# Query weights summed during K/V, and one of four gate-times-up products on GpSimd, in a fused attention and feed-forward kernel

## The chip, the core and the metric

The kernel runs on one core of a Trainium2 chip. The metric is the device time of one execution in microseconds (us). The engines are named as in the profile: PE is TensorE, DVE is VectorE, ACT is ScalarE, POOL is GpSimd, SP is SyncE, whose queue issues all DMAs here.

## What is computed

A layer norm feeds a linear attention of 32 heads and a gated feed-forward network; the attention's output is multiplied by SiLU of the feed-forward output and added to the input. There are 2048 tokens, D = 1024 and F = 3584, in bf16.

```python
xn = layernorm(x)
q, k, v = heads(xn @ wqkv)                  # 32 heads of 32
phi = lambda t: where(t > 0, t + 1, exp(t)) + 1e-6
kv = einsum("bhsd,bhse->bhde", phi(k), v);  z = phi(k).sum(over tokens)
o = (phi(q) @ kv) / (phi(q) . z + 1e-6)
s = o @ wo
f = (silu(xn @ w_gate) * (xn @ w_up)) @ w_down
out = x + s * silu(f)
```

## The kernel before, in words

**Strassen products.** All large matrix products go through one or two levels of a Strassen-like scheme with seven products in place of eight. So each block of weights needs sums and differences of its quarters before TensorE can use it. `WF` (line 607 on) holds a block: 8 KB per partition of raw weights, 8 KB of outer sums (`combos`, line 639: four operations of 128x1024) and 6 KB of inner sums (`inner`, line 648: eight operations of 128x256 or 128x512). `wload` (line 1239) issues the two DMAs of a block and its outer sums, and rotates through three raw places (`raw_at`, line 1234), three places for outer sums (`cmb_at`, line 1235) and two for inner sums. Query blocks (`q_load`) are summed on DVE, outer and inner. Gate/up blocks (`gu_load`) are summed on POOL, except the outer sums of block 0, which are on DVE.

**Stages.** (1) K/V, 0 to about 115 us of the profiled span: token tiles are normalised, transposed and multiplied with the K and V weights, and the sum of phi(k) times v is kept in PSUM. (2) Queries: two weight blocks times two halves p of the tokens, four "pairs" (`q_pair`), each with its phi (`phi_evac`, line 1035: ACT's exponential, then DVE's L1038 and L1045 or an addition). In between the K/V sum is scaled (L1210), transposed, multiplied with wo (`m_build`) and stored to DRAM as the M product; `den_run` (line 1278) makes the denominators and reciprocals, once for each half of the heads. (3) Gate/up: 14 blocks n times two token halves p, 28 pairs (`gu_pair`, line 1336), z counting them. Each product of gate and up is stored to DRAM. Beside pairs z = 3 to 10 runs `normalise` (line 1305), which divides the queries by their denominators: per call four scalings on ACT and four DVE products of 128x512 from SBUF alone. (4) The normalised queries times M, `s_pair`, from about 525 us. (5) The down projection from about 574 us, which loads chunks of the gate-times-up products (`h_load`) and multiplies with w_down; its `d_pair` makes the output.

**A pair and its four evacuations.** A pair writes a 2 x 2 arrangement of 128x512 results for gate and again for up. Three of the four are read from PSUM (kind "ps"), and one, from Strassen product 7, was first combined by DVE into an SBUF tile of f32 (kind "sb"). For gate, ACT applies SiLU; for up, line 1351 multiplies with the SiLU tile, in place and on DVE, and a DMA stores the tile.

**What sets the order.** Nothing is issued in the order of the code. Every operation becomes an `Op` of a `Plan`, with its engine, assumed duration, what it reads and writes, and the PSUM bank or temporary buffer that it takes from a pool. `schedule` (line 125) gives each a due time from TensorE's order and places them by engine, earliest start first, then due time; `emit` (line 261) writes each engine's list with the semaphore waits. A DMA that is not `asap` is also tied to a matmul some 12 us before its due time. For the planner, DVE work on SBUF alone ("port") waits for POOL. In `op` (line 460) every reader of a PSUM bank counts as a writer of it, so that two reads of a bank always follow one another with a wait, on one engine too.

**Memory.** A region from 80 KB on (`W0`) holds the weights; during K/V it also holds K/V sums, x tiles (112 to 120 KB), normalised tiles (124 to 130 KB) and phi(k) tiles. In stage 5 the same region takes chunks of products (`HC`, `HT`, `H2`: places in KB) and inner sums (`HI_AT`, `WI_AT`); `cur` (line 1618) says which chunk place each quarter takes.

The planner's calls for the two stages in question:

```python
Q[0] = q_load(0)
...
q_pair(0, 0, Q[0])
Q[1] = q_load(1)
...
G[0] = gu_load(0)
G[0].inner(IE, JG)
```

Of the kernel before, what the change touches and what calls it, by code (L numbers as in the profile page):

```python
# [9 lines left out]
ALU = mybir.AluOpType  # L10
F32 = mybir.dt.float32
BF16 = mybir.dt.bfloat16
FP16 = mybir.dt.float16
# [48 lines left out]
class Plan:  # L62
# [11 lines left out]
        self.lead = lead  # L74
        self.tag = None

    def op(self, eng, reads, writes, fn, busy, sem=None, nbytes=0, urgent=0.0, cow=None, after=None, vbs=(), asap=False):
        o = Op()
        o.eng, o.fn, o.busy, o.sem, o.nbytes, o.urgent, o.asap = eng, fn, busy, sem, nbytes, urgent, asap
        o.lat = 0.0 if sem is not None else self.LAT[eng]  # L80
        o.idx = len(self.ops)
        o.tag = self.tag
        o.port = False
        o.pad = 0.0
        o.vbs = []
        for v in vbs:
            if v not in o.vbs:
                o.vbs.append(v)
                v.ops.append(o)
        preds = set()  # L90
        for r in reads:
            for k in r.keys:
                preds.update(self.lastw.get(k, ()))
        if cow is not None:
            preds.update(cow.preds)
        if after is not None:
            preds.add(after)
        for r in writes:
            for k in r.keys:
                if cow is None:  # L100
                    preds.update(self.lastw.get(k, ()))
                    preds.update(self.readers.get(k, ()))
        for r in reads:
            for k in r.keys:
                self.readers.setdefault(k, []).append(o)
        for r in writes:
            for k in r.keys:
                if cow is None:
                    self.lastw[k] = [o]
                    self.readers[k] = []  # L110
                else:
                    self.lastw[k].append(o)
        preds.discard(o)
        o.preds = preds
        o.succs = []
        for p in preds:
            p.succs.append(o)
        o.pecum = self.pecum
        if eng == "pe":
            self.pecum += busy  # L120
            self.lastpe = o
        self.ops.append(o)
        return o

    def schedule(self):
# [58 lines left out]
        while len(order) < total:  # L184
            best = None
            for e in self.ENGS:
                a = avail[e]
                if not a:
                    continue
                t = free[e]  # L190
                lim = None
                if e == "pe":
                    n = 0
                    for o in pe_next:
                        if n >= self.window:
                            lim = o.idx
                            break
                        n += 1
                pick = None
                for o in a:  # L200
                    if lim is not None and o.idx >= lim:
                        continue
                    when, got = place(o, t)
                    if got is None:
                        continue
                    if o.port:
                        when = max(when, free["pool"])
                    if e == "pe":
                        key = (0.0, o.idx) if when <= t + 0.05 else (when, o.idx)
                    else:  # L210
                        key = (0.0, o.dl, o.idx) if when <= t else (when, o.dl, o.idx)
                    if pick is None or key < pick[0]:
                        pick = (key, o, when, got)
                if pick is None:
                    continue
                s = max(t, pick[2])
                if best is None or s < best[0]:
                    best = (s, e, pick[1], pick[3])
            if best is None:
                raise RuntimeError("no operation can go on: " + "; ".join(  # L220
                    "%s %d" % (o.eng, o.idx) for e in self.ENGS for o in avail[e][:4]))
            s, e, o, got = best
            for v, k in got:
                v.slot = k
                v.pool.free.discard(k)
                v.pool.pend.remove(o.idx)
                o.preds = o.preds | set(v.pool.users[k])
            o.start = s
            if o.sem is not None:
                free[e] = s + o.busy  # L230
                dma_free = max(s, dma_free) + o.nbytes / 310e3
                o.done = max(s + o.nbytes / 190e3, dma_free) + 1.2 + o.pad
            else:
                if o.port:
                    s = max(s, free["pool"])
                    free["pool"] = max(free["pool"], s + o.busy)
                free[e] = s + o.busy
                o.done = s + o.busy + o.lat
            for v in o.vbs:
                v.left -= 1  # L240
                if v.left == 0:
                    P = v.pool
                    P.free.add(v.slot)
                    P.time[v.slot] = max(q.done for q in v.ops)
                    P.users[v.slot] = list(v.ops)
                    P.armed[v.slot] = v.leaves
            avail[e].remove(o)
            if e == "pe":
                done.add(o)
                while pe_next and pe_next[0] in done:  # L250
                    pe_next.popleft()
            order.append(o)
            for q in o.succs:
                q.npred -= 1
                q.ready = max(q.ready, o.done)
                if q.npred == 0:
                    avail[q.eng].append(q)
# [43 lines left out]
def build_kernel(nc, A_x, A_wqkv, A_wo, B_w_gate, B_w_up, B_w_down, out, WINDOW=20, NWARM=12, NIDLE=5, LEAD=12.0):  # L301
# [9 lines left out]
    UBANK, PU = 0.0, 6.0  # L311
    RQ = lambda w, i, j, kind: kind == "ps"
    RK = lambda q, c, kind: c == 0
    N0, NA, WA = 3, 2, True
    GC0 = ("dve",) * 4
    XE0 = XE1 = XE2 = XE3 = "dve"

# [8 lines left out]
    with ExitStack() as es:  # L326
# [133 lines left out]
        def op(eng, reads, writes, fn, busy, hold=(), **kw):  # L460
            rr, rv = split(reads)
            wr, wv = split(writes)

            mine = [v for v in rv if v.pool is BANK]
            wr += [v.r for v in mine if v not in wv]
            if mine:
                kw["urgent"] = kw.get("urgent", 0.0) + UBANK
            return PL.op(eng, rr, wr, fn, busy, vbs=rv + wv + list(hold), **kw)
# [762 lines left out]
                vsem(s), 128 * KB, asap=True)  # L1231


        raw_at = [W0 * KB, (W0 + 8) * KB, R2 * KB]
        cmb_at = [(W0 + 16 + 8 * k) * KB for k in range(3)]
        inn_at = [(W0 + 40 + 6 * k) * KB for k in range(2)]
        wk = [0]

        def wload(srcs, ceng, ieng, dt=BF16, reads=()):
            k = wk[0]  # L1240
            wk[0] += 1
            rk = (0, 1, 0)[k] if k < 3 else 2 - k % 3
            f = WF(raw_at[rk], cmb_at[k % 3], inn_at[k % 2], dt)
            for q, src in enumerate(srcs):
                if not isinstance(src, list):
                    src = [(slice(0, 8), src)]
                for kts, sr in src:
                    dma(list(reads), [f.raw_r(q, range(kts.start, kts.stop))], f.v[:, q, kts], sr,
                        dsem("wr%d_%d_%d" % (rk, q, kts.start)), 512 * KB // len(src), asap=WA)
            f.combos(ceng)  # L1250
            if ieng:
                f.inner(ieng, JQ)
            return f
# [82 lines left out]
        def gu_pair(p, n, wf, at=()):  # L1336
            sgs = {}

            def evac(w, i, j, src, v, kind):
# [7 lines left out]
                if kind == "ps" and UPACT:  # L1347
                    u = tmp(H1)
                    act([v], [u], partial(vap, u, FP16), src, ACT.Identity, 512)
                    v, src, fast = u, partial(vap, u, FP16), True  # L1350
                tt([v, s], [s], partial(vap, s, FP16), src, partial(vap, s, FP16), ALU.mult, 512, fast)
                dma([s], [named("h", p, f)], h_scr[p, f][:, n * 512:(n + 1) * 512], partial(vap, s, FP16), vsem(s),
                    128 * KB, asap=True, cow=hcow(p, f))
            ST.pair(Pair(Prov(wf, XV[p]), evac, JG), at)
# [68 lines left out]
                tt([x[1], y[1]], [z[1]], z[0], x[0], y[0], alu, (hi - lo) * 512, True)  # L1423


        HC = [80, 112, 199, 96, 87]
        HT = [119, 122.5, 103, 106.5]
        H2 = 103
        HI_AT = [73.5, 75.25, 77, 94, 110, 129.5, 194, 195.75]
        WI_AT = [70, 160, 163.5, 126, 119, 122.5]  # L1430
        gone = [VB(F2, only=k) for k in range(2)] + [VB(H1, only=k) for k in range(8, 12)]
        GB = 3584

# [3 lines left out]
        def hpart(o, w, lo=0, hi=14):  # L1437

            keys = []
            for n in range(lo, hi):  # L1440
                keys += (SB.reg(o * KB + n * 512, 512) if w is None else SB.reg(o * KB + n * 512 + w * 256, 256)).keys
            v = hchunk(o)[:, lo:hi]
            return (v if w is None else v[:, :, w * 128:(w + 1) * 128]), Region(keys)

# [139 lines left out]

        for z, (n, p) in enumerate(order):
            at = []
            if z == 0:
                at.append(partial(den_run, 1))
            gu_pair(p, n, G[n], at)
            if z == 0:  # L1590
# [24 lines left out]
                G[15 + u].inner(IS, JS)  # L1615
        ST.flush()

        cur, spare = [0, 2, 1, 3], 4

        def load(q, f, c):  # L1620
            if q < 4:
# [120 lines left out]
```

## Time and profile before

| what | value |
|---|---|
| median of 13 runs | 748.37 us (745.8 to 751.18) |
| the profiled execution, its own time | 750.71 us |
| span of the profiled execution | 749.0 us |
| granted TensorE clock, mean | 0.991 |
| busy: PE, DVE, ACT, POOL | 713.4, 588.1, 380.4, 260.6 us |

The span is what the profile covers, and the execution's time is 1.7 us longer. Busy time is the time in which an engine has at least one instruction under way. A row of a group gives line, engine, operation, output and inputs with shapes, how many, busy time and mean ns of one, and then the engine's idle time just before these instructions with what ended most of it. Since helpers record operations, most tensor operations have the line of the helper: L424 (matmuls), L474 (ACT), L482 (two-tensor operations on DVE and POOL). A row of the timeline gives start, duration, engine, line, operation and how many were merged, and in brackets the idle time before it and its releaser.

### The profile page before, as it was taken

The page shows a single profiled execution, that of the slowest core. Times are in us where ns is not written, and L with a number is a line of the kernel's source. Part 1 is how long each engine was busy: PE and PEld are TensorE (multiplying, and loading weights), DVE is VectorE, ACT ScalarE, POOL GpSimd, SP SyncE. Part 2 cuts the span into 40 slices and gives each one's busy share as a digit, 9 for nine tenths or more (in the row PEclk, how much of TensorE's full clock was granted, in tenths as well). Part 3 has the DMA queues.
Part 4 walks back from the last instruction along what each step waited for, and adds up shares of the span by engine and source line. Part 5 has one row for each costly group of instructions (what it writes and reads, how often), then busy time and mean ns, then how long its engine had stood idle before and what let it go on. Part 6 is the DMA issues. An engine that isn't in the chain of part 4 may idle for free.

```text
span 749.0 us, 11806 instructions
## 1 busy us (share of the span) xinstructions
PE 713.4 (95%) x4247; PEld 399.8 (53%) x4247; DVE 588.1 (79%) x1127; ACT 380.4 (51%) x729; POOL 260.6 (35%) x230
## 2 busy tenths in 40 slices
PE   8999998997898899999999999999999999999996
PEld 3444444443565555656666566656554455464642
DVE  5999665889899889888888888889978966556433
ACT  3778665886646567665455454544665122021211
POOL 2011000255528547856678655712740000000000
PEclk9999999999999999999999999999999999999998
DMA  9834205131133454467321333235699256463622
GB/s 305 200 86 102 39 0 169 58 113 32 44 117 112 155 195 138 154 231 226 106 84 59 106 99 118 90 111 169 187 323 286 71 174 202 137 197 100 187 71 70
DMA packets 141978, 101.57 MB, mean 136 GB/s; under 512 B 19040, under 2 KB 137056, under 8 KB 141920
## 3 DMA queue, kind: packets, MB, share of 16 engines
q1 hardware_dynamic: 141920, 100.82, 44.7%
q8 instruction: 33, 0.54, 0.3%
q14 instruction: 25, 0.20, 0.1%
HBM read 68.16 MB, written 29.49 MB: 130 GB/s over the span
## 4 chain that ended last, share of the span: by engine, by line
PE 70%; DVE 14%; DMA 6%; ACT 5%; issue 3%; SPq 0%; DVEq 0%; ACTq 0%
PE ps L424 70%; DVE SB L482 10%; ACT SB L474 4%; DMA SB<-h_scratch 2%; DVE ps L482 2%; DMA out_dram<-SB 1%; DVE SB L1038 1%; DMA SB<-in_A_x_dram 1%; DMA SB<-q_scratch 1%; ACT ps L474 1%; DVE SB L1045 1%; DMA m_scratch<-SB 0%; SPq L494 0%; DMA SB<-SB 0%; DVE SB L1210 0%
## 5 line engine op out<-in xcount | busy, mean ns | idle before, releaser
L424 PE MATMUL ps<-SB 128*128 128x512 f16 (+4 forms) x4126 | 704.0, 332 | 22.8 <-DVE ps L482 7.7
L424 PEld LDWEIGHTS ps<-SB 128*128 128x128 f16 (+1 forms) x4126 | 394.2, 98 | 330.4 <-DVE ps L482 17.0
L482 POOL TENSOR_TENSOR SB<-SB 128x1024 f16<-128x1024 bf16 (+3 forms) x196 | 246.3, 1283 | 234.1 <-PE ps L424 114.1
L474 ACT ACTIVATE SB<-ps 128x256 f32<-128x256 f32 (+5 forms) x443 | 234.9, 562 | 145.2 <-PE ps L424 114.5
L482 DVE TENSOR_TENSOR SB<-SB 128x512 f16<-128x512 f16 (+11 forms) x360 | 237.4, 694 | 56.0 <-ACT SB L474 23.1
L482 DVE TENSOR_TENSOR SB<-ps,SB 128x256 f32<-128x256 f32 (+2 forms) x318 | 181.6, 591 | 56.4 <-PE ps L424 44.7
L482 DVE TENSOR_TENSOR ps<-ps,SB 128x512 f32<-128x512 f32 (+1 forms) x250 | 128.1, 527 | 26.6 <-PE ps L424 16.9
L474 ACT ACTIVATE ps<-ps 128x512 f32<-128x512 f32 (+1 forms) x172 | 84.2, 491 | 123.0 <-PE ps L424 91.0
L474 ACT ACTIVATE SB<-SB 128x512 f16<-128x512 f32 (+1 forms) x68 | 42.3, 623 | 86.4 <-DVE SB L482 86.2
L1002 POOL TENSOR_TENSOR rstd<-veps,neg_half 128x1 f32<-128x1 f32 x16 | 11.6, 735 | 63.5 <-DVE veps L1001 62.3
L1038 DVE TENSOR_SCALAR SB<-SB 128x512 f16<-128x512 f16 x64 | 24.4, 393 | 11.7 <-ACT SB L474 11.5
L474 ACT ACTIVATE SB<-SB,zc 128x512 bf16<-128x512 bf16 x32 | 22.3, 717 | 6.4 <-DVE SB L482 6.4
L474 ACT ACTIVATE SB<-SB,nmr,rstd 128x1024 f16<-128x1024 bf16 x12 | 14.6, 1234 | 1.1 <-DVE nmr L1004 1.0
L998 DVE BATCH_NORM_STATS2 stats<-SB 128x6 f32<-128x512 bf16 x16 | 11.0, 688 | 3.5 <-DMA SB<-in_A_x_dram 3.4
L1045 DVE SCALAR_TENSOR_TENSOR SB<-SB 128x512 bf16<-128x512 f32 x15 | 11.6, 781 | 0.1
L999 DVE BATCH_NORM_STATS2 stats<-SB 128x6 f32<-128x512 bf16 x16 | 10.9, 683 | 0.0
L424 PE MATMUL ps<-SB,ident 128*128 128x512 f16 x17 | 5.4, 479 | 1.4 <-POOL ident L505 1.4
L453 PE MATMUL ps<-ident,SB 128*128 128x128 f16 x40 | 3.1, 220 | 3.5 <-DVE SB L1008 2.1
L1045 DVE SCALAR_TENSOR_TENSOR SB<-ps,SB 128x512 bf16<-128x512 f32 x9 | 6.1, 685 | 0.0
L453 PEld LDWEIGHTS ps<-ident,SB 128*128 128x128 f16 x40 | 2.3, 98 | 5.7 <-DVE SB L1008 3.5
L1295 DVE RECIPROCAL SB<-SB 128x64 f32<-128x64 f32 x8 | 4.4, 544 | 0.0
L424 PEld LDWEIGHTS ps<-SB,ident 128*128 128x128 f16 x17 | 1.9, 119 | 4.0 <-issue 1.9
(28 smaller groups left out, 25.2 us busy)
## 6 DMA issues: line engine op xcount, KB each, us to landing
h_scratch<-SB SPq DMA_DIRECT2D x112, 128.0 KB, 2.0
SB<-h_scratch SPq DMA_DIRECT2D x16, 896.0 KB, 6.2
SB<-in_B_w_gate_dram SPq DMA_DIRECT2D x14, 512.0 KB, 4.0
SB<-in_B_w_up_dram SPq DMA_DIRECT2D x14, 512.0 KB, 5.3
SB<-in_B_w_down_dram SPq DMA_DIRECT2D x4, 1792.0 KB, 8.6
SB<-in_A_wqkv_dram SPq DMA_DIRECT2D x12, 512.0 KB, 8.5
SB<-in_A_x_dram SPq DMA_DIRECT2D x16, 256.0 KB, 4.5
SB<-r_scratch SPq DMA_DIRECT2D x32, 128.0 KB, 2.9
```

What stands on the lines that cost most here:

```text
L424: last = h.matmul(o() if callable(o) else o, l() if callable(l) else l, r() if callable(r) else r, start=st, stop=sp, skip_group_check=True)
L453: last = h.transpose(o(), i(), ident[:, :])
L474: return op("act", reads, writes, lambda h: h.activation(ev(o), ev(i), func, **kw), n / 1200.0 + (0.055 if src == "ps" else 0.095) + (0.09 ...
L482: f = lambda h: h.tensor_tensor(ev(o), ev(a), ev(b), alu)
L998: dve([xr] + ([named("ve", 0)] if q == 1 else []), [sA], lambda h: h.bn_stats(stats[:, j, 0, :], xa[:, 0:512]), 512)
L999: dve([xr] + ([named("ve", 0)] if q == 1 else []), [sB], lambda h: h.bn_stats(stats[:, j, 1, :], xa[:, 512:1024]), 512)
L1002: pool([ver, nh_r], [rsr], lambda h: h.tensor_tensor(rstd[:, j, :], veps[:, j, :], neg_half[:, :], ALU.pow), 0.56)
L1038: dve([e], [e], lambda h: h.tensor_scalar(vap(e, FP16), vap(e, FP16), 1.0, EPS_PHI, ALU.min, ALU.add), 512, 3.84, urgent=PU).port = True
L1045: dve(reads + [e], [out_r], lambda h: h.scalar_tensor_tensor(out_ap, ev(src), 0.0, vap(e, FP16), ALU.max, ALU.add), 512, urgent=PU).port = ...
L1295: dve([ea], [ra], lambda h, q=q: h.reciprocal(vap(ra, F32)[:, q * 64:q * 64 + 64], vap(ea, F32)[:, q * 64:q * 64 + 64]), 400)
```

## The change

It has these parts. Raw places and places for outer sums are taken in another order, so that both query blocks use places that the K/V stage frees early or never uses; the DMAs of the first two blocks are no longer `asap`, and those of the second get 20 us of urgency. The "sb" product of gate and up is put on POOL. Readers of a PSUM bank on one engine no longer wait for each other; only a reader on another engine is waited for. `normalise` starts one pair later (`N0` 4), and the second `den_run` is called at pair z = 2 instead of 0 (`ZD`). Places of the last stage, and the order of the chunk places, are set anew. The planner's list of pending buffers is cleared by the first operation of a buffer, whichever operation takes it.

```diff
-    def op(self, eng, reads, writes, fn, busy, ..., vbs=(), asap=False):
+    def op(self, eng, reads, writes, fn, busy, ..., vbs=(), asap=False, solo=()):
...
+        for r in solo:
+            for k in r.keys:
+                preds.update(q for q in self.readers.get(k, ()) if q.eng != eng)
...
-                v.pool.pend.remove(o.idx)
+                v.pool.pend.remove(v.ops[0].idx)
...
-    N0, NA, WA = 3, 2, True
+    N0, NA, WA, QU, ZD = 4, 2, True, 20.0, 2
...
             mine = [v for v in rv if v.pool is BANK]
-            wr += [v.r for v in mine if v not in wv]
+            kw["solo"] = [v.r for v in mine if v not in wv]
...
-        raw_at = [W0 * KB, (W0 + 8) * KB, R2 * KB]
-        cmb_at = [(W0 + 16 + 8 * k) * KB for k in range(3)]
+        raw_at = [R2 * KB, W0 * KB, (W0 + 8) * KB]
+        cmb_at = [(W0 + 16 + 8 * k) * KB for k in (2, 0, 1)]
...
-            rk = (0, 1, 0)[k] if k < 3 else 2 - k % 3
+            rk = k % 3
...
-                        dsem("wr%d_%d_%d" % (rk, q, kts.start)), 512 * KB // len(src), asap=WA)
+                        dsem("wr%d_%d_%d" % (rk, q, kts.start)), 512 * KB // len(src), asap=WA and k > 1).urgent = QU if k == 1 else 0.0
...
-                tt([v, s], [s], partial(vap, s, FP16), src, partial(vap, s, FP16), ALU.mult, 512, fast)
+                tt([v, s], [s], partial(vap, s, FP16), src, partial(vap, s, FP16), ALU.mult, 512, fast,
+                   "pool" if kind == "sb" else "dve")
...
-        HC = [80, 112, 199, 96, 87]
-        HT = [119, 122.5, 103, 106.5]
-        H2 = 103
-        HI_AT = [73.5, 75.25, 77, 94, 110, 129.5, 194, 195.75]
-        WI_AT = [70, 160, 163.5, 126, 119, 122.5]
+        HC = [88, 111, 199, 104, 80]
+        HT = [118, 121.5, 96.75, 100.25]
+        H2 = 96.75
+        HI_AT = [73.5, 75.25, 77, 95, 128.5, 130.25, 194, 195.75]
+        WI_AT = [70, 160, 163.5, 125, 118, 121.5]
...
-            if z == 0:
+            if z == ZD:
                 at.append(partial(den_run, 1))
...
-        cur, spare = [0, 2, 1, 3], 4
+        cur, spare = [0, 2, 3, 1], 4
```

More of the change, by code (lines that the diff above doesn't have):

```diff
@@ L75, in __init__, with op @@
         self.tag = None
-    def op(self, eng, reads, writes, fn, busy, sem=None, nbytes=0, urgent=0.0, cow=None, after=None, vbs=(), asap=False):
+    def op(self, eng, reads, writes, fn, busy, sem=None, nbytes=0, urgent=0.0, cow=None, after=None, vbs=(), asap=False, solo=()):
         o = Op()
@@ L1440, in hpart @@
             for n in range(lo, hi):
[L1441 removed]
+                q = int(o * KB) + n * 512
+                keys += (SB.reg(q, 512) if w is None else SB.reg(q + w * 256, 256)).keys
             v = hchunk(o)[:, lo:hi]
```

## The prediction

> **What bounds the kernel now.** I read the page first, then the busy times by stage, then PE's own waits and the timelines around them.
> ```profile
> PE 713.4 (95%) x4247; PEld 399.8 (53%) x4247; DVE 588.1 (79%) x1127; ACT 380.4 (51%) x729; POOL 260.6 (35%) x230
> ```
> PE (TensorE) sets the time, and the change leaves its 4247 matmuls alone. So only PE's lost time can be won: 749.0 - 713.4 = 35.6 us of gaps, and stretches at a lower granted clock.
> ```profile
> 85.00:112.00 27.00, 27.00 (x153) 13.25 (x151) 16.14 (x40) 16.10 (x30) 0.00 (x0) 1.00 0.00 1
> ```
> ```profile
> 115.00:210.00 95.00, 81.19 (x512) 43.30 (x511) 81.19 (x180) 65.05 (x131) 35.04 (x28) 0.96 0.25 77
> 210.00:330.00 120.00, 112.64 (x707) 68.35 (x705) 108.62 (x197) 75.22 (x147) 73.87 (x55) 0.99 0.49 157
> 330.00:490.00 160.00, 158.06 (x1010) 97.99 (x1008) 133.06 (x235) 80.00 (x164) 107.84 (x83) 1.00 0.37 115
> 490.00:749.00 259.00, 250.45 (x1412) 136.46 (x1409) 174.34 (x290) 82.51 (x159) 29.59 (x32) 0.99 0.55 165
> ```
> Columns: stretch, its length, busy PE, weight load, DVE, ACT, POOL, clock, DMA. Gaps of PE: 13.8 us from 115 to 210 (queries, start of gate/up), 7.4 from 210 to 330 (gate/up with the normalisation), 1.9 from 330 to 490 (gate/up alone), 8.6 after that (mostly the tail), and 3.9 before 115. The clock costs more: in windows of 5 us it was 0.66 in 140-145, 0.84 and 0.82 in 175-185 and 0.66 in 260-265, so (0.34 + 0.16 + 0.18) x 5 = 3.4 us in the first stretch and 1.7 in the second. Most gaps end on DVE, so I asked what makes DVE late.
> ```profile
> L482 POOL TENSOR_TENSOR SB<-SB 128x512 f16<-128x512 f16 x56 | 66.4, 1188 | 17.5 <-PE ps L424 15.9 <-DVE SB L482 0.9
> ...
> L482 DVE TENSOR_TENSOR SB<-ps,SB 128x512 f16<-128x512 f32 x84 | 57.3, 683 | 9.8 <-ACT SB L474 9.4
> ...
> L482 DVE TENSOR_TENSOR SB<-SB 128x512 f16<-128x512 f32 x28 | 32.3, 1153 | 0.0
> ...
> L482 DVE TENSOR_TENSOR SB<-SB 128x512 f16<-128x512 bf16 x32 | 26.1, 841 | 0.0
> ```
> The x84 and x28 rows are the same gate-times-up product; only the source differs. From PSUM it takes 683 ns, from SBUF 1153 on average, though the undisturbed ones take 0.68 too. The timelines show why:
> ```profile
> 422.57 0.69 DVE L482 TENSOR_TENSOR SB<-ps,SB 128x512 f16<-128x512 f32 x1 [0.52 <-ACT SB L474]
> 423.18 2.64 DVE L482 TENSOR_TENSOR SB<-SB 128x512 f16<-128x512 f32 x1
> 425.74 1.61 DVE L482 TENSOR_TENSOR SB<-ps,SB 128x512 f32<-128x512 f32 x3
> ...
> 418.98 11.31 POOL L482 TENSOR_TENSOR SB<-SB 128x1024 f16<-128x1024 bf16 x7 [7.38 <-DMA SB<-in_B_w_up_dram]
> ...
> 427.41 2.78 PE L424 MATMUL ps<-SB 128*128 128x256 f16 x18 [0.57 <-DVE SB L482]
> ```
> While POOL runs its weight sums, the SBUF-only product of 0.68 us lasts 2.64; the PSUM work behind it starts 2 us late, and PE waits 0.57. The same picture, larger, in the queries:
> ```profile
> 170.39 5.35 DVE L1038 TENSOR_SCALAR SB<-SB 128x512 f16<-128x512 f16 x7
> 175.67 1.63 DVE L1045 SCALAR_TENSOR_TENSOR SB<-SB 128x512 bf16<-128x512 f32 x1
> ...
> 170.56 9.06 POOL L482 TENSOR_TENSOR SB<-SB 128x512 f16<-128x512 f16 x8 [0.86 <-DVE SB L482]
> ...
> 177.97 5.77 PE L424 MATMUL ps<-SB 128*128 128x512 f16 x24 [3.20 <-DVE ps L482]
> ```
> Seven operations that start 0.2 us apart elsewhere take 5.35 us against eight of POOL, and PE stands still for 3.2 us and resumes at the lower clock.
>
> **The change part by part.** The sum is made on the profiled run: span 749.0, time 750.71, which is 2.3 us above the median 748.37; the difference is then taken off the median.
>
> *Query weights early.* The second query block's sums are 4 operations of 0.60 us and 8 of 0.20 (start to start): 4.0 us of DVE, now behind the K/V phase at 124-146. They move to 85-112, where DVE is busy 16.1 of 27 us and PE never waits; 10.9 us cover them, so 0 there (without that cover they would cost up to 4.0). Their four DMAs, and the first block's, come onto SP's queue behind the last x transpose (81.5 us) and ahead of the wo load (111.9); in between SP issues nothing, and DMA share is 0.00. Before, the first block's loads, and those of gate/up block 1, were issued at 13-24 us, among x loads; taking them out can only help the start: 0 to -0.5, taken 0. Gate/up block 0 takes the place in the queue that query block 1 had (114.6 and 120.9 us), block 1 now comes among the stores of the M product. It is used past 210 us, so 60 us hide it.
>
> *What this frees from 115 to 210.* (a) The transposes of the K/V sum wait 1.45 us for L1210, behind three query sums of 0.6; one gate sum and one small op now stand there: -1.0 (0 to -1.45). (b) At 137-141 PE waits 0.92 and 0.86 for ACT, which waits for a buffer whose store lasted 3.6 us, and the clock falls (1.7 us): 3.5 in all. Buffers come free sooner with 4 us less DVE work: -1.5 (0 to -3.5). (c) The 3.20 us stall, 1.17 and 0.41 behind it and 1.7 of clock: 6.5. POOL runs the inner sums of gate/up blocks 0 and 1, sixteen, nearly without a gap from 163 to 180. In the changed order block 0's eight come while the first query pair is evacuated, before block 1's sums start. Half the obstacle is left and the four sums of gate block 0 (2.4 us of DVE) are also gone: -4.0 (+1 to -6.5). (d) The second denominator's wait (1.59 at 202) moves two pairs later, where fewer exponentials are left: -1.0 (+0.5 to -1.6). Sum -7.5.
>
> *What it puts back there.* Block 0's inner sums, 4 x 0.67 + 4 x 1.16 = 7.3 us of POOL, now lie among the query evacuations at 130-150, where POOL has two sums of 2.1 so far. Here the Trainium skill ("SBUF — State Buffer", section "SBUF: two separate sides") speaks against the change: VectorE work with two SBUF inputs or in a two-port mode and GpSimd work lock each other out of a shared port pair for the whole instruction. By the rule at its worst all 7.3 us are DVE delay. By the row it is less: 5.35 - 7 x 0.2 = 3.95 us for 9.06 of POOL, that is 3.2, minus the 2 that the moved sums cost there now (one operation at 138 lasted 2.11). Half of the rest reaching PE, plus block 1's four sums of 2.1 moving from 138-157 to later: I take +2.5 (0 to +7). Stretch: -5.0.
>
> *The product on POOL.* 28 operations leave DVE (32.3 us) and join POOL. No row has POOL with an f32 input at this size; nearest is x56, 1188 ns, so 28 x 1.19 = 33.3 us. The skill's "GPSIMD Engine Reference", section "Engine selection", advises against such a move: two-input elementwise work is about twice as slow there. By it the price is 2 x 0.68 = 1.37, 38 us on POOL for 19 saved on DVE; by the rows it is 33 for 32. The difference is the waiting the rule leaves out. It is off PE's path either way: what waits for it is a store to DRAM and a 1 KB buffer. Behind it on POOL wait weight sums. Per block of 23.4 us POOL works some 16 and then 18.3; it is idle 7.4 of them for the next weights, so the cover is 5. From 330 to 490: the five gaps of 0.3 to 0.7 follow products of 2.2 to 2.6 us, and no other SBUF-only DVE work is left in this stretch: -1.7 of 1.9 (-0.5 to -2). From 210 to 330: DVE is relieved of 8.8 us (9 products) of 108.6, but the 32 normalisation products (841 ns, 0.41 undisturbed) stay and meet a POOL that is busier by 2.4 in 23.4: 0.43 x 32 x 16% = 2.2 us more. Of 7.4 + 1.7: -3.0 (+2 to -7). At 530.8 a matmul starts only 0.5 us after POOL's sum that it needs, and a product now stands ahead of that sum: +0.6 (0 to +1.2).
>
> *The rest.* Reads of one bank by one engine no longer wait for each other: 107 of ACT's 227 waits on itself and 40 of DVE's go; about 0.1 us each on engines with slack: -0.4 (0 to -1.5). The new chunk addresses and chunk order of the last stage keep the same releases: 0 (-1.8 to +1.8, the largest gap there, at 622).
>
> Sum: -5.0 - 1.7 - 3.0 + 0.6 - 0.4 = -9.5. Profiled run 741.2; against the median 748.37: 738.9.
>
> **Rivals.** *The waits only change place.* DVE's lock with POOL hits the phi and normalisation work as it hit the product. Then only 330-490 (-1.7) and part (a) (-1.0) stay: 745.7. For it: the 841 ns row. Against it: POOL's total between 130 and 180 is the same, while DVE's falls.
> *All of it goes:* -7.5 with (c) at its full 6.5 (-2.5), 210-330 at -7, 330-490 at -1.9: -18.9; with the 0.6 at 530 and 1 of price in the queries -17.3: 731.
> *Slower: POOL in the query phase.* The eight inner sums at 130-150 hold exponentials, buffers stay full, ACT stops, PE pauses long enough to lose its clock, and each such pause costs 1.7 on top. At the worst +7 there, two clock losses +3.4, (b) and (c) not won; left are -1.0 -1.0 from (a) and (d), -1.7 and -0.4; the normalisation +2 and 0.6 at 530: net +8.9. I take half way to that end, +4: 752. It decides once the stretch from 115 to 210 loses 4.5 us more than the 17.2 it loses now (the other parts give 1.7 + 3.0 + 0.4 - 0.6). The two stalls at 138 and 174 show that this chain exists.
> *The change doesn't do what it says:* the loads come too late for K/V. The order of the changed program puts both sums before the first query pair, so this is folded into the second rival.
>
> **How the numbers follow.** Forecast 50% (738.9, own range 734 to 744), waits change place 20% (745.7), all gone 12% (731), slower 18% (752). A measurement of this kernel can tell about 0.2%, 1.5 us, from no change. Faster by more: 0.50 + 0.12 + 0.12 of the second = 0.74; within: 0.07; slower: 0.19 (1 point from the second). Range 731 to 750: half of the third case and two thirds of the fourth are left out.
>
> **What would show it.** No SBUF-only f32 product on DVE, 28 on POOL near 1.2 us; no gap after it in 330-490; DVE busy near 555; L1038's mean (393 ns now) below 330; PE's gaps in 115-210 near 9 us with at most one dip of the clock; in 210-330 near 5. It is wrong if L1038's mean rises or PE waits for POOL.

## The result and the profile after

The changed kernel takes 742.7 us (median of 11 runs, 739.96 to 745.66) against 748.0 of the kernel before in the same comparison: ratio 0.9932, 95% interval 0.9916 to 0.9948, so 5.1 us less. In a second comparison (e1 below) the same kernel gave 0.9899 (0.9887 to 0.9912), 7.6 us less. The two intervals don't touch; what differs there is told at the end. Predicted were 738.9 us, 9.5 us less.

The busy times of the profiled execution (span 743.3 us, its own time 745.05):
```profile
PE 711.1 (96%) x4247; PEld 400.2 (54%) x4247; DVE 559.3 (75%) x1099; ACT 374.5 (50%) x729; POOL 286.1 (38%) x258
```
DVE has 28 instructions and 29 us less, POOL 28 more and 25.5 us more. The same stretches as before (length, PE, weight load, DVE, ACT, POOL, clock, DMA, GB/s):
```profile
85.00:112.00 27.00, 27.00 (x150) 12.98 (x148) 17.89 (x42) 15.57 (x30) 0.00 (x0) 1.00 0.29 78
```
```profile
115.00:210.00 95.00, 83.18 (x511) 45.02 (x509) 77.50 (x172) 65.64 (x136) 40.41 (x32) 0.98 0.27 83
210.00:330.00 120.00, 114.70 (x759) 70.95 (x757) 100.75 (x185) 75.05 (x150) 87.02 (x67) 1.00 0.48 149
330.00:490.00 160.00, 157.59 (x1014) 98.56 (x1013) 121.12 (x232) 79.36 (x167) 112.99 (x92) 1.00 0.39 122
490.00:743.00 253.00, 244.22 (x1362) 132.55 (x1360) 165.89 (x273) 78.54 (x152) 31.57 (x35) 0.99 0.56 167
```
The early query weights cost nothing in the first row: PE is still busy for all of the 27 us, and the DMA share there rose from 0.00 to 0.29. PE's gaps are 11.8 us in the queries (13.8 before), 5.3 in the normalisation (7.4), 2.4 in gate/up alone (1.9) and 8.8 to the end (8.6). The third and fourth figures did not fall, although no gap is left between 331 and 480 us. The groups by form, busy and mean ns of one:
```profile
L485 POOL TENSOR_TENSOR SB<-SB 128x512 f16<-128x512 f32 x28 | 33.0, 1179 | 26.8 <-DVE SB L485 12.9 <-ACT SB L477 10.8 <-PE ps L427 3.0
L485 DVE TENSOR_TENSOR SB<-SB 128x512 f16<-128x512 bf16 x32 | 24.9, 812 | 0.0
...
L1041 DVE TENSOR_SCALAR SB<-SB 128x512 f16<-128x512 f16 x64 | 22.0, 351 | 9.2 <-ACT SB L477 9.2
```
The product costs 1179 ns on POOL, as forecast (1.19). The third row, at 393 ns before, is taken up below. Where the time came back shows in PE's timeline at the turn to the normalised queries, and then in DVE's:
```profile
525.77 3.63 PE L427 MATMUL ps<-SB 128*128 128x512 f16 x20
530.82 1.04 PE L427 MATMUL ps<-SB 128*128 128x512 f16 x4 [1.42 <-DVE ps L485]
532.35 7.91 PE L427 MATMUL ps<-SB 128*128 128x256 f16 x36 [0.49 <-DVE ps L485]
```
```profile
523.98 1.44 DVE L485 TENSOR_TENSOR SB<-SB 128x2048 f16<-128x2048 f16 x1
527.78 2.37 DVE L485 TENSOR_TENSOR SB<-SB 128x1024 f16<-128x1024 f16 x3 [2.36 <-DMA SB<-q_scratch]
```
DVE stands idle for 2.36 us, waiting for a load, and then makes three outer sums of normalised queries in a row. The combination that PE needs comes behind them. Before, PE ran here without a break.

### The profile page after: what moved, and what is told of

The parts are those of the page before. It is cut to its first block, busy times and chain, and to the rows that moved or that the text cites. A ratio compares the mean times of both kernels' runs of the same rounds, so it can differ in the third digit from the quotient of the medians.

```text
span 743.3 us, 11833 instructions
## 1 busy us (share of the span) xinstructions
PE 711.1 (96%) x4247; PEld 400.2 (54%) x4247; DVE 559.3 (75%) x1099; ACT 374.5 (50%) x729; POOL 286.1 (38%) x258
## 4 chain that ended last, share of the span: by engine, by line
PE 78%; DVE 11%; DMA 5%; ACT 3%; issue 1%; SPq 0%; DVEq 0%
PE ps L427 78%; DVE SB L485 6%; ACT SB L477 3%; DMA SB<-h_scratch 2%; DVE ps L485 1%; DMA SB<-in_A_x_dram 1%; DVE SB L1041 1%; DMA SB<-SB 1%; DVE SB L1048 1%; DMA out_dram<-SB 1%; ACT ps L477 1%; DMA SB<-q_scratch 1%; SPq L497 0%; DVE SB L1213 0%; DVE stats L1001 0%
## 5 line engine op out<-in xcount | busy, mean ns | idle before, releaser
L485 POOL TENSOR_TENSOR SB<-SB 128x512 f16<-128x512 f16 (+5 forms) x224 | 272.0, 1247 | 203.2 <-PE ps L427 77.9
L485 DVE TENSOR_TENSOR SB<-SB 128x512 f16<-128x512 f16 (+9 forms) x332 | 206.0, 655 | 59.5 <-ACT SB L477 19.1
L485 DVE TENSOR_TENSOR SB<-ps,SB 128x512 f16<-128x512 f32 (+2 forms) x318 | 181.9, 593 | 68.4 <-PE ps L427 53.3
L1041 DVE TENSOR_SCALAR SB<-SB 128x512 f16<-128x512 f16 x64 | 22.0, 351 | 9.2 <-ACT SB L477 9.2
L477 ACT ACTIVATE SB<-SB,nmr,rstd 128x1024 f16<-128x1024 bf16 x12 | 14.6, 1236 | 1.2 <-DVE nmr L1007 1.1
```

Source lines behind the costliest of these rows:

```text
L477: return op("act", reads, writes, lambda h: h.activation(ev(o), ev(i), func, **kw), n / 1200.0 + (0.055 if src == "ps" else 0.095) + (0.09 ...
L485: f = lambda h: h.tensor_tensor(ev(o), ev(a), ev(b), alu)
L1041: dve([e], [e], lambda h: h.tensor_scalar(vap(e, FP16), vap(e, FP16), 1.0, EPS_PHI, ALU.min, ALU.add), 512, 3.84, urgent=PU).port = True
```

## Delay by stage, the measure of the experiments

Stages shift between runs, so windows of time compare badly. From each trace I took, for all 4247 matmuls, the time from start to start beyond the undisturbed one of their size (0.216 us at 512 columns, 0.109 at 256, 0.056 at 128), and cut by matmul work done: 100 us is the end of K/V, 200 the end of the queries, 320 that of the normalisation, 480 to 500 the turn to the normalised queries. Stretches of doubled spacing are counted apart, as half clock; some 3 us of that column stand even in executions without any loss of the clock after their first 7 us (e1, e5, e11). The table has one profiled execution each. The runs e1 to e4 were made on one chip, e5 to e8 on a second and e9 to e12 on a third, always beside the kernel before. Across chips only ratios are compared, and the two rows of the kernel after show that such a ratio can be off by 0.3%, some 2.5 us.

| run | ratio to before | K/V | queries | normalisation | gate/up | turn | to the end | half clock |
|---|---|---|---|---|---|---|---|---|
| before | 1 | 3.3 | 17.1 | 9.1 | 3.2 | 0.0 | 3.4 | 7.1 |
| after | 0.9932 | 3.6 | 14.5 | 8.0 | 1.3 | 2.5 | 1.9 | 5.8 |
| e1 after again | 0.9899 | 3.3 | 14.6 | 7.9 | 0.9 | 2.6 | 2.1 | 2.8 |
| e2 product on DVE | 0.9959 | 5.9 | 13.1 | 8.8 | 3.3 | 0.3 | 2.8 | 4.0 |
| e3 queries late | 1.0008 | 3.7 | 19.3 | 8.4 | 0.7 | 2.7 | 2.1 | 6.9 |
| e4 slow query reads | 0.9884 | 3.4 | 14.5 | 7.9 | 0.0 | 0.1 | 2.9 | 4.4 |
| e5 product alone | 0.9954 | 1.9 | 17.0 | 8.0 | 1.0 | 2.9 | 3.8 | 2.8 |
| e6 denominator first | 0.9948 | 4.1 | 17.8 | 7.8 | 0.0 | 0.1 | 2.7 | 5.5 |
| e7 inner sums 0 on DVE | 0.9895 | 3.1 | 12.0 | 8.9 | 0.0 | 0.1 | 1.7 | 6.0 |
| e8 inner sums 0 to 6 on DVE | 0.9840 | 5.4 | 6.2 | 10.5 | 0.0 | 0.1 | 4.2 | 4.9 |
| e9 inner sums 0, 1 on DVE | 0.9791 | 4.7 | 6.4 | 7.4 | 0.0 | 0.0 | 3.2 | 4.6 |
| e10 short POOL sums | 0.9821 | 2.9 | 12.4 | 4.4 | 0.0 | 0.1 | 3.7 | 4.6 |
| e11 e8 with short sums | 0.9764 | 3.3 | 6.8 | 4.9 | 0.0 | 0.1 | 3.9 | 3.2 |
| e12 old bank rule | 0.9906 | 1.9 | 14.9 | 7.3 | 0.1 | 0.1 | 3.9 | 4.9 |

## The experiments

My theory after the result: each part acts in its own stage about as forecast, and what is missing was lost at the turn, in DVE's queue behind a load. Rivals: the forecast's gains in the queries were never there; or the product's wait is only passed on.

**e1, the kernel after once more.**

> The changed kernel once more, nothing edited. Theory A (every gap has its cause in the order of the queues): the gaps of PE come back at the same places, 4 to 5 us lost between the last gate/up pair and the first pair of normalised queries (near 527-534), none after the product from SBUF in the pure gate/up stage, 16 to 17 us in the query stage. Theory B (the gaps are accidents of one execution): the 5 us there are absent or under 2, and others turn up. Time 742.7 by both, within 1.5.

741.4 us, 0.9899 (0.9887 to 0.9912). But for two near 1 us (at 5 and at 480 us), the gaps of more than 1 us are at the same places as in the first profile; the half clock is 3.0 us less. The turn loses 2.6 us and not the 4 to 5 expected, because the clock loss behind its gap is absent. The places are properties of the program; whether the clock falls behind a pause differs from one execution to the next.

**e2, the product back on DVE.**
```diff
-                tt([v, s], ..., ALU.mult, 512, fast, "pool" if kind == "sb" else "dve")
+                tt([v, s], ..., ALU.mult, 512, fast)
```


> The changed kernel with the product from SBUF back on DVE; the order is the same up to the first gate/up pair. Theory A (DVE work on SBUF alone is held by POOL): the five gaps of 0.3 to 0.7 us after the product come back in pure gate/up (+3), the normalisation stage loses 2 to 3 more, the product's mean is near 1.1 us; at the turn to the normalised queries 2 to 4 less is lost, because DVE is busier there and its sums for the third block stand later: 745 to 746. Rival (the gain is all from the query stage): as the changed kernel or faster, 739 to 742.7.

745.43 us, 0.9959 (0.9942 to 0.9976), 4.5 us more than e1 by the ratios. The gate/up gaps are back (3.3 us), the turn loses 0.3 instead of 2.6, and the queries lose 1.5 less. So the product on POOL is what pays in gate/up, and it is also what brings the loss at the turn and some of the price in the queries. These gaps alone do not make up the 4.5 us: with the normalisation's 0.9 they come to -0.5. Some 1.5 us can be put down to the clock, whose mean over all runs is 0.996 here and 0.998 in e1 (an estimate, 0.002 x 745); this profile also loses 2.6 us more in K/V, ahead of the first product. The remainder is not explained.

**e3, query weights late.**
```diff
-        raw_at = [R2 * KB, W0 * KB, (W0 + 8) * KB]
-        cmb_at = [(W0 + 16 + 8 * k) * KB for k in (2, 0, 1)]
+        raw_at = [W0 * KB, (W0 + 8) * KB, R2 * KB]
+        cmb_at = [(W0 + 16 + 8 * k) * KB for k in range(3)]
...
-            rk = k % 3
+            rk = (0, 1, 0)[k] if k < 3 else 2 - k % 3
...
-                        ..., asap=WA and k > 1).urgent = QU if k == 1 else 0.0
+                        ..., asap=WA)
```
The chunk places of the last stage (`HC` to `WI_AT`, `cur`) are the old ones too.

> The changed kernel with the places of weights, the rotation, the load times and the places of the last stage as before; the product on POOL, the free reads of one bank and the later normalisation and denominator stay. Theory A (early sums free DVE in the query stage): the query stage loses 20 us of PE again in place of 16.6: +3.5, 746. Rival (the query stage gained by the freer bank reads): it keeps 16 to 17, 742 to 743.

749.41 us, 1.0008 (0.9992 to 1.0024): 8 us more than e1, and no gain over before is left. The queries' gaps are 19.3 us against 14.6, and the transposes wait 1.45 us again. The theory that the query part brings nothing falls. Part of the 8 us is the clock: its mean over the 12 runs is 0.992, against 0.998 in e1, some 4.5 us as an estimate. And e3 keeps the later denominator, the later normalisation and the new bank rule, and with late weights these seem to cost: e5, which has none of them, has 17.0 us there and is 4 us faster by the ratios. They were not separated.

**e4, the planner told that query reads take 3 us longer.**
```diff
-                    dma(list(reads), ...).urgent = QU if k == 1 else 0.0
+                    d = dma(list(reads), ...)
+                    d.urgent = QU if k == 1 else 0.0
+                    d.pad = 3.0 if dt == FP16 else 0.0
```


> The changed kernel; its planner now assumes that a load of normalised queries lands 3 us later, so that the first sum of the third such block stands behind the combination that PE waits for, and not ahead of it. The order is the same up to there. Theory A (DVE waits there for a load with PE's work queued behind it): the 5 us of lost time at the turn fall to 1 or less: 738.5. Rival 1 (it is POOL's product ahead of POOL's inner sums): the loss stays, 742.7. Rival 2 (sums placed later starve the next pair): a new gap of 2 to 4 us near 540.

740.18 us, 0.9884 (0.9871 to 0.9897). The loads of the third block are now issued at 519.5 and 521.3 us instead of 521.2 and 522.9. DVE's timeline, then PE's:
```profile
522.33 3.58 DVE L485 TENSOR_TENSOR SB<-SB 128x2048 f16<-128x2048 f16 x3
525.83 0.69 DVE L485 TENSOR_TENSOR ps<-ps,SB 128x512 f32<-128x512 f32 x1
```
```profile
519.79 10.42 PE L427 MATMUL ps<-SB 128*128 128x512 f16 x59
```
DVE has no wait for a load, the combination starts at 525.83, and PE runs on. The turn loses 0.1 us instead of 2.6 and the time is 1.1 us shorter by the ratios, less than the 2.5 of this stage: in the profile of e4 the end (0.8) and the half clock (1.6) lost more than in that of e1. The two intervals overlap, so the gain in time is not clear of noise, and 740.18 misses the 738.5 of theory A. That the loss was DVE's wait for data ahead of PE's combination is shown by the trace. Both the earlier loads and the new order of DVE's queue came with this setting; which of them would have been enough is open. The runs from e6 on all carry this setting.

**e5, the product alone, on the kernel before.**

> The kernel before, with one part of the change alone: the product of the block that is read from SBUF on GpSimd (and the planner's line for reserved buffers that goes with it). Query weights, bank rule, second denominator and chunk addresses as before. Theory A, each part acts in its own stage: the normalisation stage loses about 8 us instead of 11, gate/up alone about 0 instead of 2.3, the queries stay at the 20 of before or a little over, and at the turn to the normalised queries DVE's queue stands at loaded blocks that are not there yet; the planner puts three sums of the third block ahead of PE's combination here, against one in the kernel after, so 4 to 6 us are lost there against 0.2. Sum -3 -2.4 +4 to +6 on 748.9: 747.5 to 750, no gain. Theory B, the product's gain rests on the query weights having gone early, which empties DVE: the normalisation and gate/up stages then lose as much as before, and the time is above 751.

744.7 us, 0.9954 (0.9937 to 0.9972): a gain of 3.4 us where I expected none. The gaps are near those of theory A (normalisation 8.0, gate/up 1.0, turn 2.9 and not 4 to 6), and against before these three stages come to -0.4 us. The half clock is 4.3 us less than in the profile of before, but this is an accident of the two executions profiled: over all runs of the comparison the mean clock is 0.995 for both kernels (12 and 21 runs). So the product alone makes the kernel faster, and where most of the 3.4 us come from is not shown. With e2 this makes a square: product alone -3.4, everything else alone -3.1, together -5.1 or -7.6. Within the spread of these comparisons the parts add up.

**e6, the second denominator at the first pair, `N0` 3 and `ZD` 0, on e4.**
```diff
-    N0, NA, WA, QU, ZD = 4, 2, True, 20.0, 2
+    N0, NA, WA, QU, ZD = 3, 2, True, 20.0, 0
```


> The kernel after with the slow-read setting of the e4 run, and with the second denominator's matmuls at the first gate/up pair, and the first normalisation one pair earlier, as before the change. Theory A, the prediction's step (d): the move is worth 1.0 us, so this run takes 741.2 against the 740.2 of e4, with a wait for the denominator near 200 us. Theory B: at 200 us PE waits anyway, 2.2 us, for a phi product on DVE that GpSimd's weight sum stretches to 2.3 us, and not for the denominator; moving it wins nothing: 739.8 to 740.6.

743.59 us, 0.9948 (0.9928 to 0.9968), 4.8 us more than e4 by the ratios, on another chip; both theories missed. PE's, DVE's and POOL's timeline in e6, then PE's in e4:
```profile
200.41 1.90 PE L427 MATMUL ps<-SB,Zh 128*32 128x256 bf16 x32 [3.90 <-DVE SB L485]
```
```profile
197.43 3.73 DVE L485 TENSOR_TENSOR SB<-SB 128x512 bf16<-128x512 f16 x3
```
```profile
190.40 12.78 POOL L485 TENSOR_TENSOR SB<-SB 128x1024 f16<-128x1024 bf16 x9 [14.35 <-DMA SB<-in_B_w_up_dram]
```
```profile
202.72 1.48 PE L427 MATMUL ps<-SB 128*128 128x256 f16 x9 [2.03 <-DVE SB L485]
```
The last phi products are stretched by POOL in both. With the denominator at the first pair PE needs all of them and waits 3.90 us; two pairs later it waits 2.03 at this place for other work. The clock fell to 0.50 for 6.8 us around the longer wait. Since the normalisation was put back together with the denominator, what each of the two is worth is not separated.

**e7, e8, e9: inner sums of gate/up blocks on DVE instead of POOL, on e4** (block 0; blocks 0 to 6; blocks 0 and 1).
```diff
-        G[0].inner(IE, JG)
+        G[0].inner(("dve",) * 8, JG)
...
-                G[n + 1].inner(IE, JG)
+                G[n + 1].inner(("dve",) * 8 if n < LAST else IE, JG)
```
`LAST` is 6 in e8 and 1 in e9; e7 has the first edit only.

> The kernel after with the slow-read setting of e4, and with the eight inner sums of gate/up block 0 on VectorE instead of GpSimd (by the rows 4 x 0.2 + 4 x 0.43 = 2.5 us of DVE for 7.3 us of POOL, in 130 to 165 us). Theory A, what the change puts back in the query stage is the lock between these sums and DVE's evacuations: the gap of 2.3 us at 147 and the half clock behind it (1.2 to 1.7 us) go, 736.7 to 738.2 against 740.2. Theory B, DVE has no room between 130 and 165 us, and 2.5 us more work delay the same matmuls as much as the lock did: 739.7 to 742.

> As e7, and the inner sums of gate/up blocks 1 to 6 on VectorE too, so that GpSimd runs only outer sums and products through the normalisation. Theory A, the gaps of 1.2 to 2.2 us at 173, 254, 257, 276 and 330 us come from GpSimd's inner sums, which let one DVE operation through each: they go, the normalisation products fall from 0.81 us to below 0.6, and the time is 733 to 736. Theory B, DVE is the scarce engine: it is busy 101 of the 120 us from 210 to 330, and 5 blocks x 2.5 us more bring it to 113; PE then waits for DVE everywhere: 741 to 745.

> As e8, but only gate/up blocks 0 and 1 have their inner sums on VectorE; those of blocks 2 to 6 are on GpSimd again. Theory A, the gain of e8 over e4 (ratio 0.984 against 0.988) comes from the query stage alone, where PE's delay at 180 us of work is 15 us against 24, and e8 gave 5 us back in the normalisation, whose delay grew by 13 us against 8: this run has e8's query stage and e4's normalisation, ratio 0.976 to 0.980 against the kernel before. Theory B, the query stage's gain is given back at 186 to 195 us as in e7, because the phi products left over then meet GpSimd's outer sums: 0.985 to 0.989.

e7 took 739.92 us (0.9895, 0.9867 to 0.9923), e8 735.7 (0.9840, 0.9814 to 0.9865), e9 732.94 (0.9791, 0.9762 to 0.9819). The gap at 147 in the kernel after: PE's, DVE's and POOL's timeline:
```profile
150.00 6.18 PE L427 MATMUL ps<-SB 128*128 128x256 f16 x25 [2.14 <-DVE ps L485]
```
```profile
146.47 1.37 DVE L485 TENSOR_TENSOR SB<-SB 128x512 bf16<-128x512 f16 x1
147.76 1.63 DVE L1048 SCALAR_TENSOR_TENSOR SB<-SB 128x512 bf16<-128x512 f32 x1
```
```profile
142.35 6.50 POOL L485 TENSOR_TENSOR SB<-SB 128x512 f16<-128x512 f16 x6 [1.23 <-DVE SB L485]
```
Six inner sums without a break let about one DVE operation through each. In e9, with POOL idle from 140 to 152, PE and DVE at the same place:
```profile
148.46 7.60 PE L427 MATMUL ps<-SB 128*128 128x512 bf16 x38 [0.29 <-ACT SB L477]
```
```profile
147.46 0.68 DVE L1048 SCALAR_TENSOR_TENSOR SB<-SB 128x512 bf16<-128x512 f32 x1
```
1.63 us became 0.68, and PE waits 0.29. e7 shows that one gap gone is not yet time won: its queries lose 2.5 us less than those of e4, but what is left over then meets POOL's outer sums at 186 to 192 us (a phi product and a sum of x last 2.3 us each on DVE, and PE waits 1.40 and 2.04), and its time is that of e4 within the intervals. With block 1 too (e9) the queries lose 6.4 us instead of 14.5, and the time is 7 us below e4 by the ratios, as theory A had it. That this is not the change of chip is shown by e12, a kernel near e4 on the chip of e9: e9 is 8.0 us below it. e8's time fell into theory A's range for the wrong reason: it won in the queries only, and lost 10.5 us of gaps and 2.9 of clock in the normalisation.

**e10, e11: each outer sum on POOL as two of half the length, on e4 and on e8.**
```diff
-                    tt([a[1], b[1]], [o[1]], o[0], a[0], b[0], alu, 1024, True, eng[n])
+                    if eng[n] != "pool":
+                        tt([a[1], b[1]], [o[1]], o[0], a[0], b[0], alu, 1024, True, eng[n])
+                        continue
+                    for w in range(2):
+                        half = [x[0][:, w:w + 1] for x in (o, a, b)]
+                        tt([a[1], b[1]], [o[1]], *half, alu, 512, True, eng[n])
```


> The kernel of e4, with each outer sum on GpSimd (1024 elements, 2.13 us) as two of 512 (1.2 us each by the rows), so GpSimd works 52 x 0.27 = 14 us more in all. Theory A, a VectorE operation with both inputs in SBUF waits as long as the GpSimd instruction that runs beside it, so its longest waits halve: the gap of 2.2 us at 200 falls to about 1; those at 147, 173, 254 and 330 us stand beside inner sums of 1.2 us and stay. Ratio 0.986 to 0.988 against 0.988 of e4. Theory B, what counts is GpSimd's whole working time, which grows: 0.989 to 0.992.

> The kernel of e8, with each outer sum on GpSimd as two of half the length. Theory A, e8's remaining waits of PE at 266, 291 and 322 us (2.0, 3.0 and 2.4 us, the last two with half the clock for 2 us behind them) come from two GpSimd sums of 2.1 us in a row, each of which holds one normalisation product for 1.9 to 2.3 us: with halves the products wait 1.2 us, and the gaps and clock losses shrink by 4 to 6 us: ratio 0.976 to 0.979. Theory B, DVE is full there with the inner sums (some 113 of 120 us) and PE's waits are its queue: 0.983 to 0.987.

e10 took 734.7 us (0.9821, 0.9795 to 0.9848), e11 729.82 (0.9764, 0.9737 to 0.9791). The wait at 291 us in e8, in DVE's and PE's timeline:
```profile
289.96 4.12 DVE L485 TENSOR_TENSOR SB<-SB 128x512 f16<-128x512 bf16 x2
```
```profile
294.48 5.81 PE L427 MATMUL ps<-SB 128*128 128x256 f16 x26 [2.84 <-DVE SB L485]
```
The same two products and the same matmul in e11:
```profile
287.73 2.24 DVE L485 TENSOR_TENSOR SB<-SB 128x512 f16<-128x512 bf16 x2
```
```profile
290.36 3.42 PE L427 MATMUL ps<-SB 128*128 128x256 f16 x18 [0.96 <-DVE SB L485]
```
Two products took 4.12 us beside two sums of 2.1 us, and 2.24 beside sums of half that length, while the same elements are summed in more POOL instructions. POOL's busy time rose, from 285.0 us in e4 to 293.8 in e10 and from 232.7 in e8 to 241.8 in e11, and the time fell. So the length of POOL's instruction sets the wait here, not POOL's working time. On one chip, e10 is 6.2 us below e12 and e11 11.1. e11 came out as theory A had it; part of its gain over e8 is the clock (mean 0.999 against 0.995 over all runs, some 3 us as an estimate). e10's gain is 3 us beyond my range: I had put the gaps at 254 and 330 us down to inner sums alone, and they too shrank (1.55 to 0.68, 2.0 to 0.9), so outer sums had their part in them. e11 is the fastest version, 12.9 us below the kernel after by the two medians (different chips), 1.7% by the ratios, or 1.4% below e1.

**e12, readers of a bank on one engine wait for each other again, on e4.**
```diff
-            kw["solo"] = [v.r for v in mine if v not in wv]
+            wr += [v.r for v in mine if v not in wv]
```


> The kernel of e4, with readers of one PSUM buffer on one engine again waiting for each other through a semaphore, as before the change. Theory A, the prediction's term of 0.4 us for dropping these waits: ratio 0.9885 to 0.9895 against 0.9884 of e4, a little busier waits of ACT on itself. Theory B, the waits lie in ACT's and DVE's slack and are worth nothing: the same as e4, and the same delay of PE in every stage within 0.5 us.

740.94 us, 0.9906 (0.9882 to 0.9931), against 0.9884 (0.9871 to 0.9897) of e4: the intervals overlap, and PE's delay sums to 33.2 us in the profile of e4 and 33.1 in this one, though K/V and the end differ by more than the 0.5 us that theory B allowed. A worth of 0.4 us can't be told from none.

## Why the prediction was right, and where it was off

The direction, the range (731 to 750) and the mechanism of the main parts held; 4.4 us of the 9.5 are missing in the first comparison, 1.9 in the second. One reason lies in the profile that the sum was built on. Its mean clock is 0.991, with three losses of 1.7 us that the terms drew upon; over the 53 runs of the kernel before in the later comparisons the mean is 0.995, so that a typical execution has some 3 us less to win (an estimate, 0.004 x 748). I had taken the difference off the median all the same. Step by step:

**K/V, 0.** Right: PE has no gap between 85 and 112 us. K/V's delay differs by 0.3 us, which is less than between other pairs of runs.

**Queries, -5.0.** Gaps and clock together gave -3.7 (20.3 to 16.6), -5.3 in e1. The sum is near, its terms are not all, so part of the fit is luck. (a), the transposes' wait: 1.45 to 0.76 us, -0.7 for -1.0. (b), 137 to 141 us: the two gaps of 1.1 and 1.0 and the half clock (1.7) are gone, -3.8 for -1.5. (c), at 174: 3.4 to 2.2 us, the 1.3 at 183 to 0.8, and the half clock of 1.7 gone, -3.4 for -4.0. (d), the denominator, forecast at -1.0: the gap at 200 us is 2.2 against 1.75, so nothing was won against before. It is no longer the denominator that waits, but DVE's stretched phi product ends the wait all the same; e6, which undoes the move together with the later normalisation, has 3.3 us more of gaps in this stage. The price, +2.5: the new gap of 2.3 us at 147 and, in one of the two profiles, the half clock behind it (2.1), so +2.3 or +4.4. Its mechanism, POOL's inner sums amid the evacuations, is what e7 and e9 show. The remaining half of the obstacle in (c) was worth more than anything else here: block 1's inner sums, moved away in e9, bring another 5.6 us of gaps.

**Normalisation, -3.0.** 11.0 to 8.0 with its clock: -3.0. Gaps alone fell by 1.1 and the half clock by 1.9, and a clock loss comes in some executions only (e2 has one here at 277 us, e1 none), so the exact fit is luck. Among the gaps is a new one at 330 us, by the last normalisation products, which POOL's work stretches:
```profile
326.74 3.92 DVE L485 TENSOR_TENSOR SB<-SB 128x512 f16<-128x512 bf16 x4
```
```profile
332.05 3.17 PE L427 MATMUL ps<-SB 128*128 128x256 f16 x23 [1.44 <-ACT ps L477]
```
It is absent before, in e2 with the product on DVE, and in e6 with the earlier normalisation, but also in e12; its cause was not isolated. On average the 32 products (841 to 812 ns) are no slower, so the 2.2 us that they were to lose to a busier POOL did not come; e11 halves the POOL sums and they take 631.

**Gate/up alone, -1.7.** The five gaps behind SBUF products are all gone and none is new between 331 and 480 us: -1.9 with the gap of 1.05 us at 480, which stands in this stage's column, -3.2 in e4 where that one is absent too.

**The matmul at 530, +0.6.** This is the step that failed, by its mechanism and by its size. I looked at POOL's slack of 0.5 us ahead of one matmul. What came was DVE: emptied of the product, it has in the plan room for an outer sum of a later query block ahead of PE's combination, and the sum's data were not there. That cost 2.5 us of gaps and 1.5 of half clock, 4.0 in all (2.6 in e1), and e4 took the gaps away. The forecast had asked for every engine what stands behind an added operation, but not what the planner puts into the place of a removed one, and whether its load has landed.

**Bank reads, -0.4,** not told apart from 0. **Last stage, 0:** -1.5 in this profile (the gap at 622 is gone), within its bounds.

The measured terms are -3.7 - 3.0 - 1.9 + 4.0 - 1.7 (the end with its clock), and +0.9 at the start: -5.4 of delay, against -5.7 of span. **The rival "waits only change place"** named the right lock, and what is left of PE's delay in the queries and the normalisation is this lock, as e9, e10 and e11 show; but the parts that it left out of its sum did come. **The rival "slower"** happened in small: a pause at 147 us with a clock loss behind it. It cost up to 4.4 us where it needed more than all gains.

Of the signs that I had named, DVE's busy time (555 forecast, 559.3), the product on POOL, the empty gate/up stretch and the gaps of the normalisation (5.3) came; PE's gaps in the queries are 11.8 and not near 9. L1038's mean below 330 ns was a poor sign: it fell to 351, is 360 in e3, where the query weights are late, and goes back to 401 in e12 and 394 in e5 with the old bank rule. It goes with the bank rule more than with the time.

## What to carry to other kernels

Where a planner orders the queues, taking work off an engine moves other work forward on it: look at what would be pulled ahead of the critical operation, and whether its data come from a load whose assumed time is short. An operation on VectorE with both inputs in SBUF should, by these runs, be costed by the longest GpSimd instruction that can stand beside it (4.12 us for two products beside sums of 2.1 us, 2.24 beside halves), so short GpSimd instructions, or a few cheap sums taken back to VectorE in the crowded stage (e9, e10, e11), can bring more than moving VectorE's work to GpSimd. A profile to forecast from should have a typical mean clock, or its clock losses should be left out of the sum. Take part of a change alone before trusting its sum: here the two halves added up, but settings that go with them seem to have cost time where one half was missing (e3).

## Unexpected in the hardware

The clock losses follow no fixed length of pause. Windows of 5 us behind the gap at 147, in the kernel after and in e1, which is the same program:
```profile
150.00:155.00 5.00, 5.00 (x19) 2.36 (x20) 1.88 (x5) 2.24 (x5) 0.00 (x0) 0.66 0.42 132
```
```profile
150.00:155.00 5.00, 4.67 (x26) 2.22 (x23) 3.65 (x10) 4.62 (x10) 0.00 (x0) 1.00 0.40 130
```
After a pause of 2.1 us the clock was at 0.66 in one execution and at 1.00 in the other; in e12 a pause of 3.15 us at 145 had no loss behind it and one of 2.1 at 198 had 1.7 us. The Trainium skill ("TensorE: Matmul & The Clock Gate", section "What's actually happening") has the clock fall after an idle window of about 3.4 us that runs freely. That the losses come in some executions only fits a window that is not tied to the program; that 2.1 us are enough does not fit its length. The losses themselves have one length in these traces. The two of the kernel after:
```profile
150.20:153.61 3.41, 3.41 (x12) 1.53 (x11) 0.91 (x3) 1.09 (x2) 0.00 (x0) 0.50 0.56 177
532.49:535.90 3.41, 3.41 (x13) 1.76 (x12) 2.55 (x6) 1.86 (x5) 3.35 (x5) 0.50 1.04 344
```
At 0.50 for 3.41 us, each costs 1.7 us. The three in the profile of before last 3.41 us each too; the one of e6 at 200 us lasts 6.83, twice that.

In the profiles the half clock sums to between 2.8 and 7.1 us, so one execution's span says little about a difference of 3 us, and the medians decide. It also accounts for much of what sets the two comparisons of the kernel after apart: the mean clock over all runs is 0.996 in the first and 0.998 in the second, some 1.5 us as an estimate, and the medians are 742.7 and 741.4. The other microsecond is the kernel before, 748.0 in the first comparison and 748.94 in the second. How many losses come on average also depends on the program: on the chip of e1 (0.998, 4 runs), e3 has 0.992 in the mean of 12.
